# mLSTM attention, experts and MLP: the router's steps one unit later, scores and gate broadcasts over 128 rows

## The chip, the cores and the metric

The kernel runs on one core of a Trainium2 chip, in one launch. The metric is the device time of an execution in microseconds (us). A core has five engines, each with its own list of instructions that it works off in order: PE (TensorE, matrix products), DVE (VectorE), ACT (ScalarE), POOL (GpSimd) and SP (SyncE, which here issues most of the DMAs). They wait for each other through semaphores.

## The reference

Three things are computed one after the other: an mLSTM attention over q, k, v and gates, a mixture of experts (MoE) with one expert per token, and a dense MLP.

```
B, H, S, D = 4, 8, 768, 40                       # 4 * 768 = 3072 tokens of 320 values
for t in range(S):                               # attention, per batch and head
    m_new  = max(f_gate + m, i_gate)
    C      = exp(f_gate + m - m_new) * C + exp(i_gate - m_new) * v k^T
    n      = the same with k alone
    y[t]   = sigmoid(o_gate) * (C q) / max(|n q|, 1)
logits = x @ w_gate                              # router, 8 experts
e_idx  = argmax(logits);  gate_w = softmax(logits)[e_idx]
out    = gate_w * sigmoid(x @ w_output_gate)[e_idx] * (relu(x @ w1[e_idx]) @ w2[e_idx])   # 320 -> 1024 -> 320
h      = out @ w_in;  result = max(0.01 * h, h) @ w_out                                    # 320 -> 2048 -> 320
```

## The kernel before

**Attention.** The recurrence is computed in chunks of 128 positions. A unit is one chunk of one batch with all its 8 heads: 6 chunks x 4 batches make 24 units, in the order (0,0), (0,1), ..., (5,3). For a unit, `stage_d` (L266) broadcasts the gate sums of each head over the partitions: 8 products of `sel` with `dparts` into two PSUM tiles `pd`, and ACT takes the exponential into `pe`. `dparts` holds the 32 sums (4 batches x 8 heads) in three bf16 parts, on 96 partitions. `stage_m` (L282) lets POOL set the upper triangle of `pe` to zero. `stage_s` (L304) forms the scores, 8 products of `kTm` and `qT` into two PSUM tiles `psc`, and DVE multiplies them by `pe` into `ww`. Up to three heads of 40 values share the rows of a `qT` group, and `kTm` has zeros in the rows of the others: so a score product reads 120 rows (heads 0 to 5) or 80 (6 and 7). `stage_o` (L323) adds what comes from earlier chunks (`pin`), updates the state (`pu`, `st`), multiplies `ww` with v (`ppv`) and lets DVE form the output `hh` and its denominator. `stage_g` (L378) multiplies by the output gate on POOL and masks the state for the next chunk (`stm`). `stage_y` (L388) divides, on DVE: the result is `y`, 128 tokens x 320.

**Router.** `router.front` (L570) sends `y` to DRAM (`xd`, issued by SP) and transposes it on PE in three products into the PSUM tile `rt`; ACT copies it to `xt`. `router.logits` (L582) multiplies `xt` with the gate weights, 6 products of half the columns, and DVE copies the result to `lg`. Once the four units of a chunk have their logits, `router.pick` (L601) finds the expert of each token in 8 short DVE instructions, `router.rank` (L623) counts the tokens of each expert on PE (`pp`), `router.place` (L643) computes the slots on DVE, and `router.scatter` (L672) writes token numbers to the slots by indirect DMAs on POOL. When the slots of the first chunks are written, SP loads them back (`ms`, L1157) and POOL gathers the first expert's tokens from `xd` (`xr0a`, L999).

**Order.** Nothing is scheduled by a planner: each engine's instructions run in the order in which the program records them. The table `steps` (L414 to L429) sets this order: in turn i of the loop each step works on unit i minus its lag.

```
(4, router.front), (0, stage_d), (1, stage_m), (3, stage_g), (1, stage_v), (1, stage_s), (3, stage_y),
(5, router.rank), (2, stage_o), (4, router.logits), (4, router.pick), (0, router.scatter), (5, router.place)
```

So PE does in a turn: the transposes of unit i-4, the broadcasts of unit i, the scores of unit i-1, then `pin`, `pu` and `ppv` of unit i-2, the logits of unit i-4. DVE does `ww` of i-1, `y` of i-3, `hh` and `st` of i-2, and copies the logits. At the end of a turn come the loads of unit i+3 and at most a few side operations (conversion of weights, shifts of a table). PSUM has 8 tiles that all of these share, each free again once its last reader is done. After the loop an epilogue (L452 to L499) writes out by hand the rest of the last units, with the first products of the experts in between. The experts and the MLP follow.

Of the kernel before, what the change touches and what calls it, by code (L numbers as in the profile page):

```python
# [10 lines left out]
F32 = mybir.dt.float32  # L11
F32R = mybir.dt.float32r
BF16 = mybir.dt.bfloat16
# [6 lines left out]
P = 128  # L20
B, H, S, D = 4, 8, 768, 40
BH = B * H
# [4 lines left out]
GH = (3, 3, 2)  # L27
# [47 lines left out]
def attention(ctx, tc, qT, kT, k, v, i_gate, f_gate, o_gate, psum, ident, router, side, feed, fill):  # L75
    nc = tc.nc
    ctx.enter_context(tc.manual_schedule(engines=ORDERED))
    apool = ctx.enter_context(tc.tile_pool(name="apool", bufs=1))
    lpool = ctx.enter_context(tc.tile_pool(name="lpool", bufs=2))
# [3 lines left out]
    def ps(name):  # L83
        return psum.tile([P, 512], F32, tag="ps", name=name)
# [7 lines left out]
    NV = AHEAD + 2  # L92
    NK = AHEAD + 1
    units = [(c, b) for c in range(NC_) for b in range(B)]
    n_units = len(units)
    kTm = [apool.tile([3 * D, H, P], F32, name=f"kTm{i}") for i in range(NK)]
    qTs, ks, vs, os_ = {}, {}, {}, {}

    def cols(src, h0, h1, c, b):
        return src[b, h0:h1, :, c * P : (c + 1) * P]  # L100

    def load(i):
        c, b = units[i]
        kt = kTm[i % NK]
        for j in range(3):
            nc.sync.dma_start(
                kt[j * D : (j + 1) * D, j:H:3], kT[b, j:H:3, :, c * P : (c + 1) * P].rearrange("h d t -> d h t")
            )
        qt = qTs[i] = lpool.tile([3 * D, 3, P], F32, tag="qT", name=f"qT{i}", bufs=NV)
        nc.sync.dma_start(qt[:, 0:2], cols(qT, 0, 6, c, b).rearrange("(g h) d t -> (h d) g t", g=2))  # L110
        nc.sync.dma_start(qt[0 : 2 * D, 2], cols(qT, 6, H, c, b).rearrange("h d t -> (h d) t"))
        ks[i] = lpool.tile([P, H * D], F32, tag="k", name=f"k{i}", bufs=NV)
        nc.sync.dma_start(ks[i], k[b, c * P : (c + 1) * P])
        vs[i] = lpool.tile([P, H, VW], F32, tag="v", name=f"v{i}", bufs=NV)
        nc.sync.dma_start(vs[i], v[b, c * P : (c + 1) * P])

    def load_o(c, eng=nc.sync):
        os_[c] = lpool.tile([P, B, H, D], F32, tag="o", name=f"o{c}")
        eng.dma_start(
            os_[c].rearrange("p b h d -> p b (h d)"),  # L120
            o_gate[:, c * P : (c + 1) * P].rearrange("b p x -> p b x"),
        )
# [7 lines left out]
    keep_warm(nc, psum, blank, 12)  # L130
    for i in range(NK):
        (nc.gpsimd if i % 2 else nc.vector).memset(kTm[i], 0.0)

    load_o(0)
    open_o(0)
    load(0)
    load(1)


    resetm = apool.tile([BH, NC_, P], F32, name="resetm")  # L140
    nc.gpsimd.memset(resetm, 1.0)
    nc.gpsimd.memset(resetm[:, :, 0:1], 0.0)
    sel = apool.tile([3 * BH, BH], BF16, name="sel")
    nc.gpsimd.memset(sel, 0.0)
    for j in range(3):
        nc.gpsimd.affine_select(
            sel, sel, pattern=[[-1, BH]], compare_op=ALU.not_equal, fill=1.0, base=-BH * j, channel_multiplier=1
# [1 line left out]

    m = apool.tile([BH, S], F32, name="m")  # L150
    Dc = apool.tile([BH, S], F32, name="Dc")
    dparts = apool.tile([3 * BH, S], BF16, name="dparts")
    gT = apool.tile([P, NC_, BH], F32, name="gT")
    wT = apool.tile([P, NC_, BH], F32, name="wT")
    eT = apool.tile([P, NC_, BH], F32, name="eT")
# [103 lines left out]
    W = {}  # L259

    def stage_t(c, b):
        i = c * B + b
        u = f"{c}_{b}"
        hs = slice(b * H, (b + 1) * H)
        W[c, b] = dict(v=vs.pop(i), qT=qTs.pop(i), kTm=kTm[i % NK], kn=ks.pop(i), u=u, hs=hs)

    def stage_d(c, b):
        w = W[c, b]
        pe = w["pe"] = wpool.tile([P, H, P], F32, tag="pe", name=f"pe{w['u']}")
        for hb in range(2):  # L270
            pd = ps(f"pd{w['u']}_{hb}")
            for j in range(4):
                h = b * H + hb * 4 + j
                nc.tensor.matmul(
                    pd[:, j * P : (j + 1) * P],
                    sel[:, h : h + 1].to_broadcast([3 * BH, P]),
                    dparts[:, c * P : (c + 1) * P],
                    start=True,
                    stop=True,
                )  # L280
            for j in range(4):
                h = b * H + hb * 4 + j  # L282
                nc.scalar.activation(
                    pe[:, hb * 4 + j], pd[:, j * P : (j + 1) * P], AF.Exp, bias=gT[:, c, h : h + 1]
                )

    def stage_m(c, b):
        nc.gpsimd.affine_select(
            W[c, b]["pe"],
            W[c, b]["pe"],  # L290
            pattern=[[0, H], [1, P]],
            compare_op=ALU.is_ge,
            fill=0.0,
            base=0,
            channel_multiplier=-1,
        )
# [9 lines left out]
    def stage_s(c, b):  # L306
        w = W[c, b]
        ww = w["ww"] = wpool.tile([P, H, P], F32, tag="ww", name=f"ww{w['u']}")
        for hb in range(2):
            psc = ps(f"psc{w['u']}_{hb}")  # L310
            for j in range(4):
                h = hb * 4 + j
                nc.tensor.matmul(
                    psc[:, j * P : (j + 1) * P],
                    w["kTm"][: GH[h // 3] * D, h],
                    w["qT"][: GH[h // 3] * D, h // 3],
                    start=True,
                    stop=True,
                )
            nc.vector.tensor_mul(  # L320
                ww[:, hb * 4 : hb * 4 + 4].rearrange("p h t -> p (h t)"),
                psc,
                w["pe"][:, hb * 4 : hb * 4 + 4].rearrange("p h t -> p (h t)"),  # L323
            )
# [55 lines left out]
    def stage_g(c, b):  # L380
        so3 = os_[c][:, b]
        nc.gpsimd.tensor_mul(so3, so3, W[c, b]["hh"][:, :, 0:D])
        if c + 1 < NC_:
            nc.gpsimd.tensor_mul(
                stm[b], st[b], rowm[:, None, :, None].to_broadcast([3 * D, 3, 3, VW])
            )

    def stage_y(c, b):  # L388
        w = W.pop((c, b))
        nc.vector.tensor_mul(  # L390
            router.sink(c, b), os_[c][:, b], w["den"][:, :, None].to_broadcast([P, H, D])
        )
# [3 lines left out]
    for t in st:  # L396
# [7 lines left out]
        rowm, rowm, pattern=[[D, 3]], compare_op=ALU.is_ge, fill=0.0, base=D - 1, channel_multiplier=-1  # L404
    )
    load(2)
    router.load()
    for i in range(3, AHEAD):
# [4 lines left out]
    rest = [rest[0:2], rest[2:6], rest[6:9]] + [more[i : i + 2] for i in range(0, len(more), 2)]  # L413
    steps = [  # L414
        (0, stage_t),
        (4, router.front),
        (0, stage_d),
        (1, stage_m),
        (3, stage_g),
        (1, stage_v),  # L420
        (1, stage_s),
        (3, stage_y),
        (5, router.rank),
        (2, stage_o),
        (4, router.logits),
        (4, lambda c, b: (c, b) == units[-5] or router.pick(c, b)),
        (0, lambda c, b: router.scatter(B if c == NC_ - 1 else 1)),
        (5, router.place),
    ]  # L429
    for i in range(n_units):  # L430
        for lag, fn in steps:
# [20 lines left out]
    a, b, c, d = units[-4:]  # L452
    z = units[-5]
    fill.gather()
    stage_m(*d)
    stage_g(*b)
    stage_s(*d)
    stage_y(*b)
    router.front(*a)
    fill.dup()  # L460
    router.pick(*z)
# [662 lines left out]
def mlstm_moe_mlp(  # L1124
# [48 lines left out]
    with ExitStack() as actx:  # L1173
# [39 lines left out]
        side += [nop] * 6 + parts  # L1213
        side += [nop, both(*acts[0:2]), acts[2], nop, acts[3], both(*acts[4:6]), acts[6]]
        attention(tc, qT, kT, k, v, i_gate, f_gate, o_gate, psum, ident, router, side, feed, fill)
        load_slots(0, NJ // 2, NJ)

# [229 lines left out]
```

## Time and profile before

| | |
|---|---|
| median of 3 runs | 754.25 us (752.11 to 754.36) |
| the profiled execution: its own time, its span | 763.95 us, 762.0 us |
| busy in the span: PE, PE weight loads | 726.5 us (95%), 678.1 us |
| busy: DVE, ACT, POOL | 451.7 us (59%), 342.8 us, 400.0 us |
| attention loop and epilogue | about 8 to 190 us of the span |

The span is the profiled execution from the first to the last instruction. Its own time is 1.95 us longer, and 9.7 us longer than the median of the runs: a change is worked out against the profiled execution and then taken off the median. In the profile's first table PE is busy for nearly all of the span. Busy is not the same as fast: the clock of PE is granted by the chip, at 2.4 GHz or at 1.2 GHz, and the profile shows it as PEclk, 1.00 or 0.50 of full speed, a value between for a stretch that has both.

### The profile page before, as it was taken

To read this page: it belongs to the slowest core of one execution; us is meant where nothing else is said; L and a number is where in the kernel's file an instruction comes from. 1 tells how busy PE (TensorE), PEld (TensorE's weight loads), DVE (VectorE), ACT (ScalarE), POOL (GpSimd) and SP (SyncE) were. 2 spreads that over 40 slices of the span, in tenths; PEclk is the share of its full clock that TensorE was granted. 3 is DMA by queue.
4 is the path that set the end of the run, shared out by engine and by line. 5 is a ranking of instruction groups with operands and counts; after the bars stand their busy time and mean duration, and the time that the engine had idled before them with its cause. 6 is when DMAs were issued, how large, how long until landed. Compare 5 with 4: busy or idle time off the path is not lost. (4 is left out here: it accounts for less than half of the span.)

```text
span 762.0 us, 14569 instructions
## 1 busy us (share of the span) xinstructions
PE 726.5 (95%) x5450; PEld 678.1 (89%) x5450; DVE 451.7 (59%) x936; ACT 342.8 (45%) x736; POOL 400.0 (52%) x418
## 2 busy tenths in 40 slices
PE   8899989799999798999998999999999999999998
PEld 6799979688979697999998988988988988988998
DVE  8889978774549859567755658038038038027020
ACT  5477736432563535444655456036036036036041
POOL 8658867645476565787872537037037037037041
PEclk8899989999999899999999999999999999999999
DMA  6886777311977575776664010100100100000000
GB/s 177 236 259 171 230 199 184 92 63 28 296 259 234 186 232 177 255 243 220 171 177 137 1 52 10 51 10 11 50 11 10 50 11 10 33 12 0 24 13 17
DMA packets 61790, 87.68 MB, mean 115 GB/s; under 512 B 8396, under 2 KB 53464, under 8 KB 60440
## 3 DMA queue, kind: packets, MB, share of 16 engines
q1 hardware_dynamic: 55928, 67.43, 29.8%
q10 hardware_dynamic: 2336, 10.75, 4.1%
q0 software_dynamic: 3456, 8.58, 3.5%
q8 instruction: 43, 0.70, 0.4%
q14 instruction: 27, 0.22, 0.1%
HBM read 67.87 MB, written 19.51 MB: 115 GB/s over the span
## 5 line engine op out<-in xcount | busy, mean ns | idle before, releaser
L1364 POOL TENSOR_TENSOR g2l<-lk,g2h 128x512 fp32r<-128x512 f32 (+1 forms) x112 | 126.6, 1133 | 213.6 <-ACT g2h L1363 203.7
L1373 DVE TENSOR_TENSOR lk<-p,lk 128x512 f32<-128x512 f32 (+1 forms) x112 | 68.9, 615 | 181.1 <-ACT lk L1372 179.1
L975 PE MATMUL p<-xhm,w1h 128*128 128x512 f32 (+1 forms) x336 | 119.7, 360 | 0.0
L975 PE MATMUL p<-xhm,w1l 128*128 128x512 f32 (+1 forms) x336 | 119.3, 359 | 0.0
L986 PE MATMUL po<-w2h,g2l 128*128 128x320 f32 x384 | 118.7, 309 | 0.0
L985 PE MATMUL po<-w2l,g2h 128*128 128x320 f32 x384 | 118.7, 309 | 0.0
L984 PE MATMUL po<-w2h,g2h 128*128 128x320 f32 x384 | 118.6, 309 | 0.0
L1372 ACT ACTIVATE lk<-p 128x512 f32<-128x512 f32 (+1 forms) x112 | 60.1, 536 | 73.6 <-PE p L975 73.6
L975 PE MATMUL p<-xlm,w1h 128*128 128x512 f32 (+1 forms) x224 | 80.7, 360 | 0.0
L984 PEld LDWEIGHTS po<-w2h,g2h 128*128 128x128 f32 x384 | 72.1, 188 | 0.2
L985 PEld LDWEIGHTS po<-w2l,g2h 128*128 128x128 f32 x384 | 72.1, 188 | 0.2
L986 PEld LDWEIGHTS po<-w2h,g2l 128*128 128x128 f32 x384 | 72.1, 188 | 0.0
L975 PEld LDWEIGHTS p<-xhm,w1h 128*128 128x128 f32 x336 | 63.8, 190 | 9.3
L975 PEld LDWEIGHTS p<-xhm,w1l 128*128 128x128 f32 x336 | 63.6, 189 | 9.4
L1387 ACT COPY yo<-po 128x320 f32<-128x320 f32 x24 | 10.2, 426 | 130.7 <-PE po L986 130.7
L984 PE MATMUL po<-w2h,gh 128*128 128x320 f32 x208 | 66.5, 320 | 0.0
L985 PE MATMUL po<-w2l,gh 128*128 128x320 f32 x208 | 65.9, 317 | 0.0
L986 PE MATMUL po<-w2h,gl 128*128 128x320 f32 x208 | 65.7, 316 | 0.0
L1363 ACT CAST g2h<-lk 128x512 fp32r<-128x512 f32 (+1 forms) x112 | 61.6, 550 | 1.6 <-DVE lk L1373 1.6
L937 DVE STREAM_TRANSPOSE xtm<-x2r 32x384 f32<-32x384 f32 (+3 forms) x144 | 59.6, 414 | 2.8
L975 PE MATMUL ph<-xh,w1h 128*128 128x384 f32 (+1 forms) x168 | 60.7, 361 | 0.0
L975 PE MATMUL ph<-xh,w1l 128*128 128x384 f32 (+1 forms) x168 | 60.6, 361 | 0.0
(245 smaller groups left out, 1604.8 us busy)
## 6 DMA issues: line engine op xcount, KB each, us to landing
r<-in_moe_w_dram SPq DMA_DIRECT2D x6, 1280.0 KB
r<-in_moe_w_dram SPq DMA_DIRECT2D x7, 1024.0 KB
raw<-in_moe_w_out_dram ACTq DMA_DIRECT2D x5, 1024.0 KB
r<-in_moe_w_dram SPq DMA_DIRECT2D x16, 256.0 KB
raw<-in_moe_w_in_dram ACTq DMA_DIRECT2D x4, 1024.0 KB
v<-in_v_dram SPq DMA_DIRECT2D x24, 164.0 KB
o<-in_o_gate_dram SPq DMA_DIRECT2D x6, 640.0 KB
k<-in_k_dram SPq DMA_DIRECT2D x24, 160.0 KB
```

The lines of the kernel that those rows point to most:

```text
L937: self.nc.vector.transpose(out=xt[f, k].rearrange("p k (j t) -> p k j t", t=P)[:, :, :, t], in_=blocks[t, :, g].rearrange("p j k f -> p k ...
L975: nc.tensor.matmul(ps, a, b, start=(i == 0), stop=(i == len(seq) - 1))
L984: nc.tensor.matmul(ps, gh[:, js], wh, start=(f == 0), stop=False)
L985: nc.tensor.matmul(ps, gh[:, js], wl, start=False, stop=False)
L986: nc.tensor.matmul(ps, gl[:, js], wh, start=False, stop=(f == n - 1))
L1363: nc.scalar.copy(gh, lk)
L1364: nc.gpsimd.tensor_sub(gl, lk, gh.bitcast(F32))
L1372: nc.scalar.activation(lk, pf, AF.Copy, scale=0.01)
L1373: nc.vector.tensor_max(lk, pf, lk)
L1387: nc.scalar.copy(yo, po[:, :DM])
```

## The change

The steps of the router run one unit later: `front`, `logits` and `pick` have lag 5 instead of 4, `rank` and `place` 6 instead of 5. The loop then ends before `front` and `logits` of unit (4,3) have run, so the epilogue does both. The test that skipped the pick of that unit in the loop falls away.

Besides, all 128 rows of the array are used by two kinds of products. `dparts` and `sel` get 128 partitions instead of 96, those from 96 on zero, and `kTm` gets 128 instead of 120. The rotating `qT` tiles become five tiles `qTm` that stay, zeroed once at the start. A score product reads 128 rows, not 120 or 80; a broadcast 128, not 96. For the zeros DVE gets three fills of 128x384 and one of 32 rows of `dparts`, POOL two of 128x384.

```diff
-    kTm = [apool.tile([3 * D, H, P], F32, name=f"kTm{i}") for i in range(NK)]
-    qTs, ks, vs, os_ = {}, {}, {}, {}
+    kTm = [apool.tile([P, H, P], F32, name=f"kTm{i}") for i in range(NK)]
+    qTm = [apool.tile([P, 3, P], F32, name=f"qTm{i}") for i in range(NV)]
...
-        qt = qTs[i] = lpool.tile([3 * D, 3, P], F32, tag="qT", name=f"qT{i}", bufs=NV)
-        nc.sync.dma_start(qt[:, 0:2], cols(qT, 0, 6, c, b).rearrange("(g h) d t -> (h d) g t", g=2))
+        qt = qTm[i % NV]
+        nc.sync.dma_start(qt[0 : 3 * D, 0:2], cols(qT, 0, 6, c, b).rearrange("(g h) d t -> (h d) g t", g=2))
...
         (nc.gpsimd if i % 2 else nc.vector).memset(kTm[i], 0.0)
+        (nc.gpsimd if i % 2 else nc.vector).memset(qTm[i], 0.0)
+    nc.vector.memset(qTm[NK], 0.0)
...
-    dparts = apool.tile([3 * BH, S], BF16, name="dparts")
+    dparts = apool.tile([P, S], BF16, name="dparts")
+    nc.vector.memset(dparts[3 * BH : P], 0.0)
...
-                    sel[:, h : h + 1].to_broadcast([3 * BH, P]),
+                    sel[:, h : h + 1].to_broadcast([P, P]),
...
-                    w["kTm"][: GH[h // 3] * D, h],
-                    w["qT"][: GH[h // 3] * D, h // 3],
+                    w["kTm"][:, h],
+                    w["qT"][:, h // 3],
...
-        (4, router.front),
+        (5, router.front),
...
-        (5, router.rank),
+        (6, router.rank),
         (2, stage_o),
-        (4, router.logits),
-        (4, lambda c, b: (c, b) == units[-5] or router.pick(c, b)),
+        (5, router.logits),
+        (5, router.pick),
         (0, lambda c, b: router.scatter(B if c == NC_ - 1 else 1)),
-        (5, router.place),
+        (6, router.place),
...
     fill.gather()
+    router.front(*z)
     stage_m(*d)
     stage_g(*b)
     stage_s(*d)
     stage_y(*b)
+    router.logits(*z)
     router.front(*a)
```

**PE, the turn of unit (2,2).** The two numbers in a name are chunk and batch, the last one counts tiles. Before, the row `rt1_2` (the transposes) reads the `y` of unit (1,2):

```order
L369 MATMUL ppv1_3_1156<-v7_628,ww1_3_1004 64x41 x16
L587 MATMUL rt1_1_1098<-wg_232,xt1_1_1102 64x16 x6
L577 MATMUL rt1_2_1203<-ident_63,y1_2_1141 128x128 x3
L274 MATMUL pd2_2_0_1210<-dparts_179,sel_166 128x128
...
L313 MATMUL psc2_1_0_1234<-qT9_839,kTm1_118 128x128 x4
L313 MATMUL psc2_1_1_1240<-qT9_839,kTm1_118 128x128 x4
```

In the changed program the same place on PE, ahead of the same broadcasts `pd2_2`:

```order
L373 MATMUL ppv1_3_1128<-v7_617,ww1_3_976 64x41 x16
L593 MATMUL rt1_0_1059<-wg_240,xt1_0_1063 64x16 x6
L583 MATMUL rt1_1_1185<-ident_63,y1_1_989 128x128 x3
L278 MATMUL pd2_2_0_1192<-dparts_187,sel_174 128x128
...
L317 MATMUL psc2_1_0_1216<-qTm4_125,kTm1_118 128x128 x4
L317 MATMUL psc2_1_1_1222<-qTm4_125,kTm1_118 128x128 x4
```

The transposes and logits are those of the unit before, the rest stands where it stood. The `y` that the transposes read was recorded on DVE two turns earlier, not one.

**DVE, the pick of chunk 2.** Names as above; `mx` to `zs` are the pick, `wide_r2` is a side operation, `ww3_3` the next unit's weighting. Before:

```order
L588 COPY lg2_1351<-rt2_3_1756 128x16
L614 TENSOR_REDUCE mx_1843<-lg2_1351 128x4
L615 TENSOR_TENSOR eq_1844<-lg2_1351,mx_1843 128x32
...
L618 TENSOR_TENSOR oh_1846<-desc_443,r_1845 128x32
...
L621 TENSOR_REDUCE zs_1848<-eq_1844 128x4
L816 TENSOR_SCALAR wide_r2_1752<-wide_r2_1752 128x1024
L320 TENSOR_TENSOR ww3_3_1902<-psc3_3_0_1903,pe3_3_1762 128x512
```

And in the changed program:

```order
L594 COPY lg2_1332<-rt2_2_1733 128x16
L822 TENSOR_SCALAR wide_r2_1729<-wide_r2_1729 128x1024
L324 TENSOR_TENSOR ww3_3_1864<-psc3_3_0_1865,pe3_3_1739 128x512
...
L594 COPY lg2_1332<-rt2_3_1834 128x16
L620 TENSOR_REDUCE mx_1920<-lg2_1332 128x4
L621 TENSOR_TENSOR eq_1921<-lg2_1332,mx_1920 128x32
...
L627 TENSOR_REDUCE zs_1925<-eq_1921 128x4
L324 TENSOR_TENSOR ww4_0_1976<-psc4_0_0_1977,pe4_0_1840 128x512
```

The pick stands a unit later and ahead of `ww4_0`; the side operation stayed where it was, so the two are no longer in the same turn.

**POOL, the end of the loop.** `slots` are scatters, `pe` the masking of `stage_m`, `o` the output gate, `xr0a` the gather for the first expert. Before:

```order
L682 DMA slots_77<-meta_445,sl_2417 28672x4
L288 AFFINE_SELECT pe5_1_2445<-pe5_1_2445 128x1024
L382 TENSOR_TENSOR o4_1750<-o4_1750,hh4_3_2482 128x320
L384 TENSOR_TENSOR stm3_193<-st3_189,rowm_218 120x369
L288 AFFINE_SELECT pe5_2_2540<-pe5_2_2540 128x1024
L382 TENSOR_TENSOR o5_2194<-o5_2194,hh5_0_2577 128x320
L999 DMA xr0a_2689<-xd_78,ms_68 128x320 x2
L288 AFFINE_SELECT pe5_3_2618<-pe5_3_2618 128x1024
```

In the changed program:

```order
L292 AFFINE_SELECT pe5_1_2393<-pe5_1_2393 128x1024
L386 TENSOR_TENSOR o4_1727<-o4_1727,hh4_3_2441 128x320
L388 TENSOR_TENSOR stm3_202<-st3_198,rowm_227 120x369
L687 MEMSET gap_98 1x1
L688 DMA slots_77<-meta_450,sl_2485 28672x4
...
L292 AFFINE_SELECT pe5_2_2504<-pe5_2_2504 128x1024
L386 TENSOR_TENSOR o5_2167<-o5_2167,hh5_0_2541 128x320
L1005 DMA xr0a_2662<-xd_78,ms_68 128x320 x2
L292 AFFINE_SELECT pe5_3_2591<-pe5_3_2591 128x1024
```

The last four scatters of chunk 3, which ended ahead of `pe5_1` (the row `slots` is the fourth of them), now stand behind it, ahead of `pe5_2`; the gather keeps its place.

## Rows read from the trace of the kernel before

**Rows 1.** Windows: stretch, length, busy of PE, PEld, DVE, ACT, POOL, PEclk, DMA.
```profile
25.00:47.00 22.00, 17.52 (x247) 16.91 (x245) 21.07 (x45) 11.91 (x33) 15.39 (x16) 0.89 0.85 249
47.00:150.00 103.00, 92.74 (x1280) 89.61 (x1279) 88.42 (x254) 60.57 (x164) 73.11 (x93) 0.91 0.69 186
150.00:190.00 40.00, 37.65 (x446) 35.21 (x445) 25.65 (x111) 14.18 (x42) 20.81 (x33) 1.00 0.16 44
```

**Rows 2.** PE's timeline, one turn: start, length, instruction, count, [idle before <-releaser].
```profile
72.72 0.55 PE L577 MATMUL rt<-ident,y 128*128 128x128 f32 x3
73.55 2.00 PE L313 MATMUL psc<-qT,kTm 120*128 120x128 f32 x16
...
78.11 0.44 PE L577 MATMUL rt<-ident,y 128*128 128x128 f32 x2
```

**Rows 3.** PE's waits, 8 to 152 us: total, times, longest.
```profile
PE rt L577 <- DVE y L390: 7.5, 5, 3.2
PE pp L633 <- DVE oh L618: 4.6, 2, 3.3
```

**Rows 4.** PE's timeline, three of those five waits of rt.
```profile
31.53 0.53 PE L577 MATMUL rt<-ident,y 128*128 128x128 f32 x3 [3.23 <-DVE y L390]
...
65.70 0.63 PE L577 MATMUL rt<-ident,y 128*128 128x128 f32 x3 [1.35 <-DVE y L390]
...
140.05 0.52 PE L577 MATMUL rt<-ident,y 128*128 128x128 f32 x3 [1.84 <-DVE y L390]
```

**Rows 5.** DVE's timeline behind the wait at 65.70.
```profile
69.10 0.69 DVE L320 TENSOR_TENSOR ww<-psc,pe 128x512 f32<-128x512 f32 x1 [0.36 <-PE psc L313]
70.20 0.69 DVE L320 TENSOR_TENSOR ww<-psc,pe 128x512 f32<-128x512 f32 x1 [0.41 <-PE psc L313]
```

**Rows 6.** The windows view, three stretches with a low granted clock.
```profile
66.00:69.40 3.40, 3.40 (x22) 3.35 (x21) 2.86 (x11) 2.95 (x7) 2.76 (x4) 0.50 0.61 181
...
107.00:117.00 10.00, 9.80 (x89) 9.55 (x89) 7.75 (x27) 3.91 (x12) 3.60 (x7) 0.50 0.80 228
...
142.00:144.00 2.00, 2.00 (x11) 2.00 (x11) 1.83 (x10) 1.98 (x6) 1.10 (x3) 0.50 0.79 214
```

**Rows 7.** DVE's timeline from the pick of chunk 2 on.
```profile
105.30 1.84 DVE L618 TENSOR_TENSOR oh<-desc,r 128x32 bf16<-128x32 f32 x1
...
112.03 0.49 DVE L372 TENSOR_TENSOR hh<-hh,ppv 128x328 f32<-128x328 f32 x1 [1.07 <-PE ppv L369]
...
116.19 0.69 DVE L320 TENSOR_TENSOR ww<-psc,pe 128x512 f32<-128x512 f32 x1 [0.68 <-PE psc L313]
117.62 0.69 DVE L320 TENSOR_TENSOR ww<-psc,pe 128x512 f32<-128x512 f32 x1 [0.74 <-PE psc L313]
```

**Rows 8.** POOL's timeline beside that pick.
```profile
105.99 1.10 POOL L288 TENSOR_SCALAR_AFFINE_SELECT pe<-pe 128x1024 f32<-128x1024 f32 x1
```

**Rows 9.** The score products by line: shortest, median, longest in ns, first and last start, forms.
```profile
L313 PE MATMUL psc<-qT,kTm x384: 273/275/579, 8.9 to 160.9; 120*128 120x128 f32 x144, 80*128 80x128 f32 x48
```

**Rows 10.** The timelines of DVE and ACT at the start.
```profile
2.43 0.91 DVE L132 MEMSET kTm<- 120x1024 f32 x1 [0.16 <-issue]
...
12.92 0.69 DVE L320 TENSOR_TENSOR ww<-psc,pe 128x512 f32<-128x512 f32 x1 [1.19 <-POOL pe L288]
...
9.53 1.66 ACT L283 ACTIVATE pe<-pd,gT 128x128 f32<-128x128 f32 x6
```

**Rows 11.** The timelines of POOL, SP and PE at the end of the loop and behind it.
```profile
148.24 0.96 POOL L682 DMA_INDIRECT slots<-meta,sl  x1 [0.22 <-issue]
...
157.53 1.02 POOL L999 DMA_INDIRECT xr0a<-xd,ms  x1 [1.24 <-DMA xd<-y]
...
159.82 1.10 POOL L288 TENSOR_SCALAR_AFFINE_SELECT pe<-pe 128x1024 f32<-128x1024 f32 x1
...
151.43 0.33 SPq L1157 DMA_DIRECT2D ms<-slots  x1
...
164.41 0.25 PE L633 MATMUL pp<-oh,ones 128*128 128x8 bf16 x4 [0.45 <-DVE oh L618]
```

More of the change, by code (lines that the diff above doesn't have):

```diff
@@ L95, in attention @@
     n_units = len(units)
-    kTm = [apool.tile([3 * D, H, P], F32, name=f"kTm{i}") for i in range(NK)]
-    qTs, ks, vs, os_ = {}, {}, {}, {}
+    kTm = [apool.tile([P, H, P], F32, name=f"kTm{i}") for i in range(NK)]
+    qTm = [apool.tile([P, 3, P], F32, name=f"qTm{i}") for i in range(NV)]
+    ks, vs, os_ = {}, {}, {}
     def cols(src, h0, h1, c, b):
@@ L142, in attention @@
     nc.gpsimd.memset(resetm[:, :, 0:1], 0.0)
-    sel = apool.tile([3 * BH, BH], BF16, name="sel")
+    sel = apool.tile([P, BH], BF16, name="sel")
     nc.gpsimd.memset(sel, 0.0)
@@ L264, in stage_t @@
         hs = slice(b * H, (b + 1) * H)
-        W[c, b] = dict(v=vs.pop(i), qT=qTs.pop(i), kTm=kTm[i % NK], kn=ks.pop(i), u=u, hs=hs)
+        W[c, b] = dict(v=vs.pop(i), qT=qTm[i % NV], kTm=kTm[i % NK], kn=ks.pop(i), u=u, hs=hs)
     def stage_d(c, b):
```

## The prediction

> **What bounds the kernel now.** I read the first table of the page, then the windows by stage, PE's waits, and around each wait the timelines of PE and DVE. PE is the bound: busy 726.5 of 762.0 us. The change touches only the attention and its epilogue, about 180 us of the span; what follows keeps its instructions, so a gain or loss is one of when the experts can start. In the middle of the attention, from 47 to 150 us, PE is busy for 92.74 of 103 us and DVE for 88.42, and PE's granted clock is 0.91 on average [rows 1]. The 2.4 GHz and 1.2 GHz levels mix to 0.91 if 18% of the stretch, 18.5 us, runs at 1.2 GHz. Two engines are thus close to the bound, and PE's pace has a second enemy, its clock.
>
> PE's largest waits before 152 us are the transposes for DVE's `y`, 7.5 us in five waits, and the counting of tokens for DVE's `oh`, 4.6 us in two, one of 3.3 us [rows 3]. Of the five, three are seen in [rows 4]: 3.23 us at 31.53, 1.35 at 65.70, 1.84 at 140.05; the other two hold 7.5 - 6.42 = 1.1 us. What a wait costs is not its length but what is late behind it. A turn at full clock takes 78.11 - 72.72 = 5.39 us from transposes to transposes [rows 2]. The one that starts with the wait at 65.70 takes 72.72 - 65.70 = 7.02 us, since the clock is 0.51 between 66.0 and 69.4 [rows 6]: 1.63 us more than a turn at full clock, and DVE stands idle in it twice for the scores, 0.36 and 0.41 us [rows 5]. The clock is at 1.2 GHz again from 107 to 117 us, right behind the wait of 3.3 us, and from 142 to 144 us, behind the wait at 140.05 [rows 6].
>
> **The change part by part.**
>
> *The transposes one unit later.* They read a `y` that DVE made a turn earlier, so their wait for `y` at the head of a turn goes. Next late are PSUM tiles. A turn asks for eight and there are eight, so the second `pd` or the scores of this turn wait for a reader in the last turn: `ww`, `y` or `hh` of the same DVE. If DVE is behind, PE waits at the scores and not at the transposes, and its lead is what lies between the two: 73.55 - 72.72 = 0.83 us at most [rows 2]. DVE then finds its scores ready up to 0.83 us earlier. That is worth something only where DVE was short of scores.
> - At 31.53 DVE is busy for 21.07 of 22 us around the wait [rows 1]: the three-microsecond wait is DVE's own load, and removing it gives nothing (0 to 0.93, DVE's idle time there). I take 0.
> - At 65.70 the lead covers DVE's idle 0.36 + 0.41 us: -0.8. At most the slow clock goes as well, -0.77 - 1.63 = -2.4; at least nothing.
> - The two short waits: -0.4, between 0 and -1.1.
> - At 140.05 the wait was 1.84. The lead gives 0.83 at most, and some of the slow clock behind it goes: -1.2. Bounds are 0 and -0.83 - 1.63 = -2.5.
>
> *The pick and what follows one unit later.* The side operations keep their turns, so the pick of chunk 2 no longer shares a turn with the shift of `wide_r2`, and that of chunk 1 not with a conversion of weights. The pick is 8 instructions; `oh` alone took 1.84 us at 105.30, and ended at 107.14 just behind POOL's masking of `pe` (105.99 to 107.09) [rows 7, 8]. PE waited 3.3 us for it, and in the slow clock behind it DVE was idle for 1.07 + 0.68 + 0.74 = 2.49 us [rows 7]. How a pick meets POOL a turn later is not to be read from the trace. Bounds: nothing is gained, or all of 2.49. I take half, -1.2, since of the four picks in the loop two show this wait.
>
> The Trainium skill, "SBUF — State Buffer", section "SBUF: two separate sides", says that a DVE operation with two SBUF inputs and a GpSimd operation that reads SBUF take a shared pair of ports in turn, each for the whole instruction. The trace agrees with it at this place: 1.84 us, ending with POOL's 1.10 us. By that rule the moved pick is stretched again wherever it meets a masking, which POOL does in every turn; the term of -1.2 would be 0, the sum below -1.3 and the time 752.95; its chance is counted with that of rival B below, whose last clause it is.
>
> *128 rows.* A score product took 273 ns at least and 275 in the median, with the 144 of 120 rows and the 48 of 80 together (each recorded twice) [rows 9]: rows cost no time, so 120 to 128 costs 0, and the broadcasts' 96 to 128 likewise. Whether more rows in use change the granted clock no row here can show; 0 is taken in the sum, and the other end is rival C.
>
> *The fills.* One `kTm` fill of 1024 columns takes DVE 0.91 us [rows 10]. Three of 384 columns take 0.91 x 384 / 1024 = 0.34 us each, the one of `dparts` no more than that: 1.0 to 1.4 us in all, before the first scans. Behind them stand ACT, whose first exponential starts at 9.53, and DVE's first `ww` at 12.92, which had waited 1.19 us for POOL [rows 10]. POOL gets two more fills as well. Most is covered by ACT's own start: +0.3, between 0 and +1.4.
>
> *The tail.* The last four scatters of chunk 3 stand one masking later. They ended at 148.24 + 0.96 = 149.20, the slots were loaded back from 151.43, and the gather followed at 157.53; it had waited 1.24 us for `xd`, the copy of `y` that `front` of unit (4,3) sends [rows 11]. That `front` now stands behind the gather, so this wait goes, and the wait for the slots takes its place. POOL was ready for the gather at 157.53 - 1.24 = 156.29. A turn's delay is 5.39 us. Of it 1.24 us is covered by the wait that goes; how much more depends on when the slots had landed between 151.43 and 156.29, which no row shows. If only at 156.29, 5.39 - 1.24 = 4.15 us is late; if within 0.7 us of the issue, nothing. Below zero the end is -1.24, if the gather is earlier by the wait that goes. I take +0.8: it means that the load took 1.5 us, a third of the stretch. Late here is the masking of (5,3) behind the gather, 159.82 [rows 11], and with it the last `ww`. PE also does the transposes and logits of (4,3) in the epilogue, at most 0.55 us for the three transposes [rows 2] and about as much for the small logits; the loop has one turn's fewer, so this is moved, not added, and part of it lies in idle time like the 0.45 us at 164.41 [rows 11].
>
> *Sum.* -0.8 - 0.4 - 1.2 - 1.2 + 0.3 + 0.8 = -2.5 us. On the profiled execution's own time of 763.95 that is 761.4. Its span of 762.0 and its own time lie 9.7 us above the median of the runs, 754.25, so the prediction is 754.25 - 2.5 = 751.7 (rounded down from 751.75).
>
> **The rivals.**
>
> B, *the waits only change their place.* DVE is busy for 88.42 of 103 us [rows 1] and PE cannot be ahead of it by more than eight PSUM tiles allow. Then each wait for `y` turns up at the scores, the clock falls as before, and the pick is stretched as before. For it: PE's two largest groups of waits are for DVE [rows 3]. Against it: DVE itself waited for PE behind two of the places [rows 5, 7]. What remains is 0 in the middle and between -1 and +1 at the ends: 754.0. That the change does not do what it says belongs here.
>
> C, *the clock stays up.* With more rows in use, and no wait at the head of the turns, the granted clock stays at 2.4 GHz where it fell behind the waits. The slow stretch of 3.4 us from 66.0 to 69.4 [rows 6] cost 1.63 us, 0.48 us for each microsecond. Both short stretches and half of the ten microseconds from 107 on give -1.63 x 2 - 0.48 x 5 = -5.7; with -1.0 for waits, 747.5. For it: each of the three falls has a wait ahead of it. Against it: the clock is also low in 107 to 117 while PE is busy for 9.80 of 10 us [rows 6], and no row shows that rows in use matter.
>
> D, *the gather is late.* The scatters of chunk 3 end after the masking of (5,1) instead of ahead of it. If the slots land later than POOL comes to the gather, the masking of (5,3) behind it is late, and with it the last `ww` and `ppv` on DVE and PE. It decides from the point where the load needs more than the 0.7 us of slack that the sum of 4.86 (from 151.43 to 156.29) and 1.24 leaves over a turn of 5.39 us. Its full price is 4.15, that is 3.35 more than the forecast holds, and a PE that stands still so long falls to 1.2 GHz as it did behind the waits of [rows 4], 1.63 us more: 751.7 + 3.35 + 1.63 = 756.7. For it: a turn of delay is more than any wait in this stretch covers. Against it: POOL has the four scatters ahead of the gather now, so it comes to it later itself.
>
> **How the numbers follow.** My forecast, 751.7, has a chance of 0.40, and its own range is 749.5 to 753.5; B 0.22, C 0.18, D 0.20. About 0.3%, 2.3 us, is what a measurement of this kernel can tell from no change: below 752.0 is faster, above 756.5 slower. Faster is then 0.26 of the forecast's 0.40, since it lies near the bound, and all of C: 0.44. Slower is 0.11 of D, 0.07 of B and 0.04 of the forecast: 0.22. The same is the rest, 0.34. The best of all bounds gives -2.4 - 1.1 - 2.5 - 2.5 = -8.5, or 745.8, and 1.24 less with the tail; the worst is +1.4 + 4.15 + 1.63 = +7.2, or 761.4. The range of 745.5 to 757.0 leaves out both far ends, which need all terms at the same end, and holds the four cases.
>
> **What would show it.** In the profile of the changed kernel the waits of the transposes for `y` are gone, and instead shorter ones of `pd` or the scores for DVE stand at the same turns; if they sum to 7.5 us again, B holds. The clock by windows between 47 and 150 us is above 0.91 if C holds, and the stretch from 66 on is the first to look at. DVE's `oh` tells of the pick: below 0.3 us in all four, the term was right. The gather waits for the slots, and the last `ww` comes 0 to 1 us later relative to the last scores; 3 us or more is D. The forecast is wrong if PE's clock falls at other places, where one of 3.4 us costs 1.63 us, or if the fills delay ACT's first exponential by their full length.

## The result: 1.3% slower, and the profile after

The changed kernel took 765.64 us in the median (762.16 to 767.73, 4 runs) against 754.31 us before (752.11 to 754.72, 4 runs): a ratio of 1.0132, with a 95% interval of 1.0097 to 1.0167 (the two medians alone give 1.0150). The forecast was 751.7 us, the range 745.5 to 757.0. The profiled execution took 762.16 us, its span is 760.0 us. The kernels ran on several chips, on which the kernel before takes 754 to 757 us or 762 to 764 us; each ratio below is to the kernel before on the same chip.

PE's waits from 8 to 152 us in the changed kernel (total, times, longest), which answer to [rows 3]:

```profile
PE pp L639 <- DVE oh L624: 10.1, 4, 4.3
PE pd L278 <- DVE ww L324: 3.1, 2, 2.9
PE psc L317 <- DVE ww L324: 1.9, 2, 1.7
PE pu L354 <- DVE count L674: 1.4, 2, 1.3
```

The transposes wait for `y` no more; `pd` and `psc` wait in their place, as foretold (the two longest, 2.9 and 1.7 us, stand before 47 us). Not foretold is the first row: the counting of tokens (`pp`) waits 10.1 us for the pick's `oh`, where it waited 4.6. Two of the four waits make 8.6 of it. PE's timeline shows them, at the picks of chunks 1 and 3:

```profile
87.58 0.26 PE L639 MATMUL pp<-oh,ones 128*128 128x8 bf16 x4 [4.29 <-DVE oh L624]
...
139.19 0.26 PE L639 MATMUL pp<-oh,ones 128*128 128x8 bf16 x4 [4.27 <-DVE oh L624]
```

DVE's timeline says why `oh` is late there. Its short operations on 128x32 take 0.19 us undisturbed; these three took 1.59, 1.85 and 3.35:

```profile
83.61 1.59 DVE L621 TENSOR_TENSOR eq<-lg,mx 128x32 f32<-128x32 f32 x1
...
85.68 1.85 DVE L624 TENSOR_TENSOR oh<-desc,r 128x32 bf16<-128x32 f32 x1
...
135.10 3.35 DVE L621 TENSOR_TENSOR eq<-lg,mx 128x32 f32<-128x32 f32 x1
```

And POOL's timeline, what it did meanwhile:

```profile
82.91 0.80 POOL L386 TENSOR_TENSOR o<-o,hh 128x320 f32<-128x320 f32 x1
83.67 0.79 POOL L388 TENSOR_TENSOR stm<-st,rowm 120x369 f32<-120x369 f32 x1
84.42 0.72 POOL L306 TENSOR_TENSOR wv<-v,wT 128x328 f32<-128x328 f32 x1
...
86.37 1.10 POOL L292 TENSOR_SCALAR_AFFINE_SELECT pe<-pe 128x1024 f32<-128x1024 f32 x1
...
134.74 1.11 POOL L292 TENSOR_SCALAR_AFFINE_SELECT pe<-pe 128x1024 f32<-128x1024 f32 x1
135.80 0.82 POOL L386 TENSOR_TENSOR o<-o,hh 128x320 f32<-128x320 f32 x1
136.56 0.81 POOL L388 TENSOR_TENSOR stm<-st,rowm 120x369 f32<-120x369 f32 x1
137.31 1.09 POOL L292 TENSOR_SCALAR_AFFINE_SELECT pe<-pe 128x1024 f32<-128x1024 f32 x1
```

Read the ends: `eq` ends at 85.20, behind `wv` (85.14); `oh` at 87.53, behind the masking (87.47); the other `eq` at 138.45, behind a masking (138.40). POOL's instructions follow each other almost without a gap (the one cut out is a scatter, 85.34 to 86.35), and DVE's operation gets through only at the end of a row of them. The Trainium skill, "SBUF — State Buffer", section "SBUF: two separate sides", has this as a lock that each instruction takes whole; the 3.35 us here shows a hold that lasts over the rest of one instruction and three more.

The stretches that answer to [rows 1], and the second slow one of PE's clock:

```profile
25.00:47.00 22.00, 17.18 (x237) 16.28 (x237) 20.26 (x43) 11.13 (x27) 16.70 (x18) 0.92 0.84 248
47.00:150.00 103.00, 90.82 (x1288) 87.39 (x1287) 92.90 (x261) 63.89 (x173) 74.80 (x92) 0.93 0.73 193
150.00:190.00 40.00, 36.97 (x444) 33.93 (x442) 24.16 (x108) 10.99 (x35) 21.73 (x34) 1.00 0.15 43
...
139.40:149.50 10.10, 10.10 (x89) 9.85 (x87) 6.14 (x24) 6.79 (x14) 3.74 (x7) 0.50 0.16 57
```

PE's clock is at 1.2 GHz from 139.4 to 149.5, right behind the wait of 4.27 us. DVE is busy for 92.90 of 103 us there, PE for 90.82: neither has much room.

### The profile page after: what moved, and what is told of

It is laid out like the page before. It is cut to its first block, busy times and chain, and to the rows that moved or that the text cites. A ratio compares the mean times of both kernels' runs of the same rounds, so it can differ in the third digit from the quotient of the medians.

```text
span 760.0 us, 14573 instructions
## 1 busy us (share of the span) xinstructions
PE 722.7 (95%) x5450; PEld 673.3 (89%) x5450; DVE 455.3 (60%) x940; ACT 342.6 (45%) x736; POOL 403.1 (53%) x420
## 5 line engine op out<-in xcount | busy, mean ns | idle before, releaser
L1393 ACT COPY yo<-po 128x320 f32<-128x320 f32 x24 | 10.2, 426 | 130.9 <-PE po L992 130.9
L1052 POOL DMA_INDIRECT x<-yo,ms x26 | 33.1, 1272 | 52.0 <-ACT yo L1046 51.3
```

The costliest lines, as they stand in the source:

```text
L1052: put = self.nc.gpsimd.indirect_dma_start(out=self.x2, out_offset=bass.IndirectOffsetOnAxis(ap=ms[:, j, 1:2], axis=0), in_=yo, in_offset=None,
L1393: nc.scalar.copy(yo, po[:, :DM])
```

## The experiments

**Which part costs.** Theory L: the moved steps. Theory R: the 128 rows, the fills, the lasting tiles. Theory C: neither, but the clock's falls. The first kernel has only the lags and the epilogue, the second only the rows and tiles:

```diff
-        (4, router.front),  ... (5, router.rank),  ... (4, router.logits), (4, ...pick), ... (5, router.place),
+        (5, router.front),  ... (6, router.rank),  ... (5, router.logits), (5, router.pick), ... (6, router.place),
```

> Only the lags and the epilogue of the change; tiles, fills and products as before. Theory L (the moved router steps cost the time: PE's wait for y comes back as a longer wait for the pick's oh, 10.5 us in five waits in the changed kernel against 4.6 in two): about 765 us, ratio 1.010 to 1.016. Theory R (the 128 rows, the fills or the lasting tiles cost it): 751 to 755, ratio 0.995 to 1.002. Theory C (neither part costs by itself; the clock's falls come elsewhere): between 754 and 762, and the granted clock goes with the time.

Measured: 765.92 us, ratio 1.0117 (1.0092 to 1.0143).

> Only the 128 rows of the change: larger zeroed tiles, lasting qTm, products over 128 rows; the lags and the epilogue as before. Theory L: 752 to 756, ratio 0.997 to 1.003. Theory R: about 765, ratio 1.010 to 1.016. Theory C: between 754 and 762, with the clock.

Measured: 754.77 us, ratio 0.9988 (0.9969 to 1.0007). Theory L holds: the steps cost all that can be told from the noise, and the rows nothing.

**Both kernels once more,** one execution of each.

> The kernel before once more, for a profile of an execution near its median of 754.3 (the one profiled took 763.95). If the profiled one was 9.7 us long by its clock, this one is 752 to 756 with a mean clock above 0.975 and fewer microseconds at 1.2 GHz between 8 and 150 us; if it was something else, the clock is the same 0.969 at 10 us less.

> The changed kernel once more, to see what varies between its executions (762.2 to 767.7). By the clock: 764 to 768 with a mean clock of 0.969 to 0.972, and falls at other places than in the first profile; otherwise the same places with the same clock.

Measured: before 755.41 us with a mean clock of 0.980, changed 765.82 with 0.969. So the profile on which the prediction rests was of an execution of another course. In the windows view of the new execution of the kernel before the clock does not fall once from 64 to 132.7 us:

```profile
64.00:132.70 68.70, 60.87 (x941) 58.68 (x939) 64.47 (x183) 43.44 (x118) 55.58 (x70) 1.00 0.76 205
```

The falls at 66 and from 107 on [rows 6] are not there, and neither is the held pick of chunk 2 [rows 7]. In the changed kernel, in turn, the clock falls at the end of each of the two long waits (4.29 us to 89.08, 4.26 to 142.64) and stays low for 10.2 us; from 47 to 150 us it is 0.97 in the kernel before (first row) and 0.88 in the changed one:

```profile
47.00:150.00 103.00, 93.09 (x1382) 89.88 (x1381) 93.30 (x274) 66.75 (x181) 77.05 (x98) 0.97 0.71 193
...
47.00:150.00 103.00, 91.81 (x1260) 88.25 (x1258) 90.42 (x256) 60.98 (x165) 72.52 (x87) 0.88 0.70 193
87.60:97.80 10.20, 8.72 (x84) 8.48 (x85) 7.72 (x25) 5.35 (x9) 3.97 (x7) 0.50 0.65 192
142.20:152.40 10.20, 9.76 (x88) 9.52 (x89) 6.72 (x28) 6.39 (x13) 3.17 (x6) 0.50 0.18 62
```

That is about 18 us more at 1.2 GHz. At the prediction's 0.48 us for each, worked out from [rows 2, 6], it makes about 9 of the 10.4 us between the two executions: an estimate, since no run here holds the clock apart from the waits.

DVE's timeline of the new execution of before, then POOL's and PE's:

```profile
102.48 0.36 DVE L615 TENSOR_TENSOR eq<-lg,mx 128x32 f32<-128x32 f32 x1
...
103.85 0.47 DVE L618 TENSOR_TENSOR oh<-desc,r 128x32 bf16<-128x32 f32 x1
...
102.71 0.80 POOL L382 TENSOR_TENSOR o<-o,hh 128x320 f32<-128x320 f32 x1
...
104.37 0.24 PE L633 MATMUL pp<-oh,ones 128*128 128x8 bf16 x4 [0.42 <-DVE oh L618]
```

and the same of the profile ahead of the prediction:

```profile
103.35 1.47 DVE L615 TENSOR_TENSOR eq<-lg,mx 128x32 f32<-128x32 f32 x1
...
102.52 0.80 POOL L382 TENSOR_TENSOR o<-o,hh 128x320 f32<-128x320 f32 x1
...
107.19 0.25 PE L633 MATMUL pp<-oh,ones 128*128 128x8 bf16 x4 [3.27 <-DVE oh L618]
```

In the new one `eq` starts 0.23 us ahead of POOL's `o`, in the old one 0.83 us behind it: PE waits 0.42 us or 3.27. One kernel, two courses. What brings the one or the other is not shown, and the chip is a rival to the offset of these two engines. In the old profile PE has three waits that nothing in the trace ends:

```profile
147.17 0.25 PE L587 MATMUL rt<-wg,xt 128*64 128x16 f32 x2 [0.19 <-issue]
147.87 0.30 PE L587 MATMUL rt<-wg,xt 128*64 128x16 f32 x3 [0.46 <-issue]
...
150.03 0.44 PE L274 MATMUL pd<-dparts,sel 96*128 96x128 bf16 x5 [0.99 <-issue]
```

From 100 to 160 us, waits of this kind stand in all nine profiles from chips on which the kernel before takes 762 to 764 us (e5 to e8, e14 to e18) and in none of the other ten. So the profile ahead of the prediction most likely comes from such a chip, on which 763.95 us is ordinary, and the median that the change was taken off from one of the others.

**Which of the moved steps.** Theories P (the pick's new turn), F (front's lead gathers the waits), W (PE's standing still before `pp`) and D (DVE's own delay). The edits are in the lags alone:

```diff
# e5: before, with
+        (5, router.pick), (6, router.rank), (6, router.place),
# e6: the lags and the epilogue of the change, with
+        (7, router.rank), (7, router.place),
# e7: before, with        (e8: the same, with the 128 rows)
+        (6, router.rank), (6, router.place),
```

> Half of the moved steps, everything else as before: pick, rank and place one unit later (lags 5, 6, 6), front and logits at lag 4 as before. Theory P (the pick in its new turn meets POOL's instructions and is held up, and PE waits 4.3 us for oh before pp at chunks 1 and 3): PE's waits before pp stay at about 8 to 10 us in all and the time is 760 to 766. Theory F (it is front's lead: PE does not wait for y any more, so its wait gathers into one long one before pp): with front back at lag 4 the waits split into rt and pp again, none over 2.5 us, and the time is 752 to 757.

Measured: ratio 1.0018 (0.9983 to 1.0052); before took 763.93 us on this chip. In its profile no wait before `pp` is over 2.3 us, as F has it. But that execution took 759.34 us, the second fastest of ten; the median of 765.29 us lies in P's range, and on such a chip the changed kernel itself comes out at 1.0024 only (e16, below). So P is not decided by this run.

> The lags and the epilogue of the change, without the 128 rows, and rank and place yet a turn later (lag 7), so that PE asks for oh a whole turn after DVE made it. Theory W (what costs is PE standing still before pp, and the slow clock behind it): no wait before pp in the loop, time 750 to 757, that is 9 to 14 us less than the lags alone. Theory D (what costs is DVE itself, held up by POOL in the pick; PE would wait for its next ww all the same): eq and oh stay at 1.6 to 3.4 us, the waits go to pd and psc, time 761 to 767.

Measured: ratio 1.0064 (1.0038 to 1.0090), 769.52 us, above the ranges of both theories; by the ratio it is nearer to D. In its trace no wait before `pp` is left in the loop, and from the first `ppv` of unit (1,0) to that of (5,0) it takes 102.7 us (before, in e3: 101.9); but then PE waits 3.40 us for the gather's tokens (`xr0a`), which come a turn later still.

> The kernel before with rank and place alone one turn later (lag 6), front, logits and pick where they were. It takes away the four waits before pp, 4.2 us in the profile of an execution of 755 us. Theory W: 749 to 754, ratio 0.992 to 0.998. Theory D: the wait moves on to ww or y, 754 to 757, ratio 0.998 to 1.002.

Measured: ratio 1.0066 (1.0030 to 1.0102): slower, against both theories. PE's timeline has the waits that were taken from `pp`, gathered at the transposes:

```profile
88.45 0.52 PE L577 MATMUL rt<-ident,y 128*128 128x128 f32 x3 [3.85 <-DVE y L390]
...
115.53 0.52 PE L577 MATMUL rt<-ident,y 128*128 128x128 f32 x3 [3.41 <-DVE y L390]
```

PE waits for DVE at one place or the other. Theory W, that to remove the wait is to win its time, falls.

> The 128 rows of the change, with the lags of the kernel before except rank and place at 6. If the rows are worth about -0.1% as measured alone and both add: 748 to 753; if the rows are worth nothing, the time of the kernel with rank and place at 6 alone.

Measured: ratio 1.0089 (1.0057 to 1.0121), as e7 within the intervals: the rows add nothing that can be told from the noise.

**What makes the wait long.** Theory K: POOL holds the pick. Theory F as before. In the kernel before (e3, first row) POOL's weight conversion `w2l` stands behind chunk 1's pick, which ends at 81.85; in the changed kernel it stands ahead of the moved pick, which starts at 83.39:

```profile
82.79 1.55 POOL L892 TENSOR_TENSOR w2l<-r,w2h 128x640 fp32r<-128x640 f32 x1 [0.69 <-ACT w2h L883]
...
80.34 1.56 POOL L898 TENSOR_TENSOR w2l<-r,w2h 128x640 fp32r<-128x640 f32 x1
```

Two edits on POOL's work, no lag touched:

```diff
# e9, e11: POOL's weight conversion (w2l) in turn 13, not 12
-        side += [nop] * 6 + parts
-        side += [nop, both(*acts[0:2]), ...
+        side += [nop] * 6 + parts[:6] + [nop, parts[6]]
+        side += [both(*acts[0:2]), ...
# e10, e11: one scatter in turn 20, not two
-        (0, lambda c, b: router.scatter(B if c == NC_ - 1 else 1)),
+        (0, lambda c, b: router.scatter(B if c == NC_ - 1 and b > 0 else 1)),
```

> The changed kernel, with the one weight conversion that POOL does (w2l, 1.56 us, recorded in turn 12) recorded a turn later. Theory K (POOL's instructions stand back to back when DVE's pick of chunk 1 comes, so its two-input operations are held for 1.59 and 1.85 us, and PE waits 4.3 us for oh): without w2l ahead POOL is done earlier, eq and oh of chunk 1 take 0.2 to 0.7 us, PE waits at most 2.3 us there and the slow clock behind it shrinks; about half of the loss comes back, ratio to before 1.004 to 1.009. Theory F (PE's lead gathers DVE's lag into one wait, whatever POOL does): the wait at chunk 1 stays above 3.5 us, ratio 1.010 to 1.016.

Measured: ratio 1.0057 (1.0039 to 1.0075). DVE's, POOL's and PE's timelines at chunk 1's pick:

```profile
84.94 0.63 DVE L621 TENSOR_TENSOR eq<-lg,mx 128x32 f32<-128x32 f32 x1
...
86.51 0.19 DVE L624 TENSOR_TENSOR oh<-desc,r 128x32 bf16<-128x32 f32 x1
...
83.95 0.81 POOL L386 TENSOR_TENSOR o<-o,hh 128x320 f32<-128x320 f32 x1 [1.19 <-DVE hh L376]
...
86.76 0.26 PE L639 MATMUL pp<-oh,ones 128*128 128x8 bf16 x4 [2.13 <-DVE oh L624]
```

Without `w2l` ahead, POOL has time to wait for DVE (1.19 us), and comes behind it in step. `oh` takes 0.19 us, and PE's wait is 2.13 us instead of 4.29 (4.25 in e10, on the same chip with this pick left as it is). This is theory K, and F's 3.5 us are missed. The changed kernel itself did not run on this chip, so "half of the loss" rests on its ratio elsewhere.

> The changed kernel, with one scatter instead of two on POOL in turn 20, the other in turn 21. Theory K: eq of chunk 3's pick, 3.35 us in the changed kernel, takes at most 1.3 us, PE waits at most 2.3 us for oh there; about half of the loss comes back, ratio 1.004 to 1.009. Theory F: the wait at chunk 3 stays above 3.5 us, ratio 1.010 to 1.016.

Measured: ratio 1.0093 (1.0057 to 1.0130), between the theories. Chunk 3's pick, on DVE and POOL:

```profile
139.36 1.05 DVE L621 TENSOR_TENSOR eq<-lg,mx 128x32 f32<-128x32 f32 x1
...
140.89 1.83 DVE L624 TENSOR_TENSOR oh<-desc,r 128x32 bf16<-128x32 f32 x1
...
139.56 0.79 POOL L388 TENSOR_TENSOR stm<-st,rowm 120x369 f32<-120x369 f32 x1
...
141.57 1.10 POOL L292 TENSOR_SCALAR_AFFINE_SELECT pe<-pe 128x1024 f32<-128x1024 f32 x1
```

The edit freed `eq` (1.05 us) and the masking then held `oh` (1.83 us, to 142.72): PE still waited 3.62 us. The hold moved, it did not go.

> The changed kernel with both edits on POOL. Theory K: both picks take less, no wait before pp above 2.3 us, ratio 0.997 to 1.004, that is most of the loss is back. Theory F: both waits stay above 3.5 us, ratio 1.010 to 1.016.

Measured: ratio 1.0045 (1.0017 to 1.0074), above K's range: chunk 1 free (2.13 us), chunk 3 not (3.62 us).

**The other half.** To free chunk 3's pick too, POOL's masking is left out for two units, with a control:

```diff
     def stage_m(c, b):
+        if c == NC_ - 1 and b < 2:
+            return
```

> The changed kernel with POOL's weight conversion a turn later, as before, and POOL's masking of the units (5,0) and (5,1) left out (2 x 1.1 us of POOL; the upper triangle of these two units is then not zeroed). Theory K: eq of chunk 3's pick, held for 3.35 us by o, stm and the second masking, is held by o and stm alone and takes at most 1.7 us; PE waits at most 2.7 us there; ratio to before 0.997 to 1.003. If the loss that is left (0.57%) is not that pick's, the wait may shrink but the ratio stays at 1.004 to 1.008.

> The control: the kernel before with the same two maskings left out. If POOL's masking costs nothing there by itself, ratio 0.997 to 1.002; if leaving it out is a gain of its own, below 0.997, and the run of the changed kernel is to be read against this one.

Measured: the control 0.9988 (0.9968 to 1.0008), so the edit itself is worth nothing; the changed kernel with both picks free 1.0081 (1.0054 to 1.0109), which misses theory K's 0.997 to 1.003. The waits are what theory K says (2.13 and 2.19 us), and the loop is back in the profile, which is of the fastest of e12's five executions (758.40 us; their median is 762.99). Between the first `ppv` of one unit and another, in us; in the first two rows the stretch holds the turn of the pick before and after the change:

| units | before (e3) | changed | changed (e4) | e9 | e12 |
|---|---|---|---|---|---|
| (2,1) to (2,3), chunk 1's pick | 13.2 | 16.5 | 16.8 | 13.4 | 14.6 |
| (4,1) to (5,0), chunk 3's pick | 23.2 | 25.6 | 25.3 | 24.1 | 19.1 |
| (1,0) to (5,0), the loop | 101.9 | 108.4 | 113.0 | 106.1 | 102.1 |
| (5,0) to (5,3), the end | 13.2 | 15.2 | 15.2 | 16.1 | 20.4 |

But the end of e12 loses what the loop won. POOL's timeline and DVE's:

```profile
155.07 1.03 POOL L1007 DMA_INDIRECT xr0a<-xd,ms  x1 [4.80 <-DMA ms<-slots]
...
157.36 1.11 POOL L294 TENSOR_SCALAR_AFFINE_SELECT pe<-pe 128x1024 f32<-128x1024 f32 x1
...
158.51 1.29 DVE L326 TENSOR_TENSOR ww<-psc,pe 128x512 f32<-128x512 f32 x2 [5.47 <-POOL pe L294]
```

The gather waits 4.80 us for the slots, the last masking stands behind it, and the last `ww` waits 5.47 us. That is rival D of the prediction, step by step. So the gather was moved behind that masking in the epilogue, and the work on its tokens behind the last `stage_o`:

```diff
-    fill.gather()
     router.front(*z)
     stage_m(*d)
     stage_g(*b)
+    fill.gather()
...
     stage_o(*d)
+    fill.dup()
+    fill.turn()
+    fill.split()
```

> The changed kernel with both picks freed as in the run of both picks (the conversion a turn later, the masking of (5,0) and (5,1) left out), and in the epilogue the gather behind the last masking on POOL and the transposes of what it brings behind the last ppv on PE. Theory KD (the loss is two pieces: the held picks in the loop, and in the epilogue the gather that waits for slots scattered a turn later, with the last masking, ww and ppv behind it): the last ww waits less than 1.5 us, and the ratio to before is 0.996 to 1.002. If the rest of the loss is not the gather, it stays at 1.005 to 1.010.

> The same, with nothing left out: the changed kernel, POOL's conversion a turn later and the epilogue with the gather behind the last masking; chunk 3's pick is still held. Theory KD: what is left is chunk 3's hold, ratio 1.000 to 1.005. Otherwise 1.005 to 1.010.

Measured: 1.0003 (0.9976 to 1.0029), and 1.0070 (1.0040 to 1.0100), which misses its expectation; before took 762.8 us on this chip. To see whether chip or edit made the difference, three versions ran together on one more chip, before 762.48 us:

> The changed kernel as it is, on the same chip as the next two. By all runs so far: ratio to before 1.010 to 1.016. If the chip matters (on the chip of the last two runs before took 763 us, not 756), below 1.008.

> Both picks free, the epilogue of the change: the gather ahead of the last masking. Theory KD: 1.004 to 1.010, as measured on another chip (1.0081).

> Both picks free and the gather behind the last masking. Theory KD: 0.996 to 1.003, at least 0.4% below the run with the picks free alone. If the gather is not the rest of the loss, the two are equal within their intervals.

Measured: changed 1.0024 (1.0001 to 1.0047), picks free 0.9963 (0.9946 to 0.9979), picks free and gather moved 1.0013 (0.9996 to 1.0031). Two things follow. To free both picks is worth 0.6% here, with intervals apart (e12 against the first measurement of the change: 0.5%, with intervals that overlap). The loop shows it in every trace: with both picks free it takes 101.8 to 106.3 us (e12, e14, e17, e18), with the lags of the change and the picks held 108.4 to 113.0 (the two profiles of the changed kernel, e1, e16). And moving the gather cost 0.5% where it was to gain: its own trace has PE waiting 3.41 us for the tokens behind the last `ppv`, and in e17's profile, the fastest of its ten executions, the gather waited only 2.46 us for the slots. So the late gather as the rest of the loss is seen in e12's trace and not confirmed by a version that is free of it.

The chip matters more than expected: the changed kernel took 764 to 766 us each time (765.64, one execution of 765.82, 763.87), and the kernel before 754 to 757 on some chips, 762 to 764 on others. Whether on the latter it has the course with the held pick of chunk 2, no trace that is known to be of the kernel before on such a chip shows; the profile ahead of the prediction (763.95 us), which bears their mark, has it, and its loop takes 109.7 us, as e16's does. No version beats both kernels on more than one chip.

## Why the prediction was wrong, point by point

- *The transposes one unit later.* Right that their wait goes and DVE's pace stays: `pd` and `psc` wait 5.0 us in its place. The lead was held to be worth up to 0.83 us at a place, and 2.4 us in all. No gain shows in the traces; PE spends the lead before `pp`: in e3 PE waited 0.50 at `rt` and 1.46 at `pp` in chunk 1's turn, in e9, where the pick is free, 2.13 at `pp` alone.
- *The pick.* This step failed, in sign. It took -1.2 us, between nothing and 2.49 of gain, and left a loss out: that POOL would hold the moved pick longer, and the slow clock behind PE's longer wait. It noted that chunk 1's pick leaves a turn with a conversion of weights, which was DVE's, and not that it comes into the one with POOL's `w2l`, which stood behind it before. The sign that it named, `oh` below 0.3 us in all four picks, failed (0.52, 1.85, 0.43, 0.19). Measured: from `ww` to the end of `oh`, chunk 1's turn took DVE 8.2 us in the changed kernel (79.35 to 87.53) and 6.0 in e3 (75.38 to 81.40). PE's wait grew from 1.96 to 4.29, and the turn with the slow clock behind it to 11.09 us, from 7.84 for the turn of e3 that has this pick. The prediction did say, as another reading, that the moved pick would be stretched again wherever it meets a masking; that named the mechanism, and its 0 was still too good.
- *The base.* The terms at 65.70 and for the pick were read from falls of the clock and a hold that the execution near the median (e3) does not have. The text noted that the profiled execution was 9.7 us above the median, and took its terms from it all the same. So part of what it meant to win was not there to be won. (Two slips without weight: the clock from 66.0 to 69.4 is 0.50 in [rows 6], not 0.51, and it is the execution's own time that lies 9.7 us above the median, its span 7.75.)
- *128 rows, 0.* Right: 0.9988 for them alone, and the score products take 274 to 276 ns as in [rows 9].
- *The fills, +0.3.* Right: four fills of 0.38 us on DVE, and ACT's first exponential at 9.76 us where [rows 10] has 9.53.
- *The tail, +0.8.* Too small. From (5,0) to (5,3) it takes 1.9 us more than in e3. POOL's and SP's timelines of the changed kernel:

```profile
156.90 1.03 POOL L1005 DMA_INDIRECT xr0a<-xd,ms  x1 [3.04 <-DMA ms<-slots]
...
153.88 0.33 SPq L1163 DMA_DIRECT2D ms<-slots  x1
```

The wait for `xd` [rows 11] has given way to one for the slots, as foretold; from the issue of their load to the gather it takes 3.02 us, where the prediction took 1.5. The last `ww` starts 1.8 us behind the last scores, 0.1 in e3: later than the forecast's 0 to 1, short of D's 3.
- *The rivals.* B was nearest in mechanism (the waits come back at `pd`, `psc` and `pp`, the pick is held again) and priced it at nothing. C is out: the clock of the changed kernel from 47 to 150 us, 0.93 in the first profile, is above the 0.91 of [rows 1], which was C's sign, but it is 0.88 in e4, and both are below the 0.97 of e3. D named the piece of the end; it had not the larger piece in the loop.

Settled by runs: that the steps cost it (e1, e2), that POOL holds the picks of chunks 1 and 3 and PE waits for them (e9 to e12), and that the loop is 2 to 11 us shorter with both picks free (trace against trace, on several chips), worth 0.6% of the time on one chip (e16, e17). Open: why e12, with both free, still loses 0.8% on a chip where the kernel before takes 756 us, how that divides between slots and clock, and why the kernel before differs by chip.

## What to carry to other kernels

Before a term is taken from a stall, see whether the profiled execution is like those of which the median is: one that lies 1.3% above it, here probably from another chip, has stalls that the others lack. Where two engines hold each other up, as POOL holds DVE here, moving a step by a turn changes which instructions meet; price the short operations of the moved step at the length of what the other engine does back to back, not at their own. And a wait that is taken away from an engine with a lead can come back at the next thing that it asks of the engine behind it, as PE's for DVE did here and in e7.

## What was not expected of the hardware

A DVE operation of 0.19 us took 3.35 us, because POOL had the rest of one instruction and three more in a row. And the same program had two courses 8.5 us apart (763.95 and 755.41 us): in one DVE's `eq` starts 0.83 us behind POOL's `o`, in the other 0.23 ahead. Whether that offset or the chip makes the difference is open.
